# A different form of phi, one load moved behind another, and sums shifted between engines, in a fused linear-attention and SwiGLU kernel

## The chip, the cores and the metric

The kernel runs on one core of one Trainium2 chip. The metric is the device time of one execution in microseconds (us); smaller is better. A profile's *span* is some 1.8 us shorter than the time of the same execution. All runs quoted here are fast (granted TensorE clock 0.995 to 1.0), and every kernel is compared with runs of the kernel before that were taken in the same rounds on the same chip.

Names of engines: PE is the matrix engine, PEld its weight loads, DVE the vector engine, ACT the scalar engine, POOL the general-purpose engine, SP the engine that issues plain DMAs.

## The reference

```python
def phi(x):                       # elu(x) + 1
    return np.where(x > 0, x, np.exp(x) - 1.0) + 1.0
q_p, k_p = phi(q), phi(k)         # q, k, v: [8, 8, 576, 64]
kv  = einsum('bhsd,bhse->bhde', k_p, v)
z   = sum(k_p, axis=2)
num = einsum('bhsd,bhde->bhse', q_p, kv)
den = einsum('bhsd,bhd->bhs', q_p, z)[..., None] + 1e-06
x   = (num / den) as [4608, 512]
out = (silu(x @ w_gate) * (x @ w_val)) @ w_out     # d_ff = 1536
```

The two forms of phi are equal: relu(x) + min(exp(x), 1), and min(max(x, 0) + 1, exp(x)).

## The kernel before

The 4608 tokens are worked through in nine groups of 512 (`g` = 0 to 8), each with a gate/value product (L1) and an output product (L2). Batch b+1's attention is done in the gaps of group b. PE is the engine to keep busy; the rest must be ready in time. Group 0 is special: its weights are still arriving, so its L2 runs in sixteen blocks `i`, each with a third or a sixth of the contraction (`f0` to `f1`), and batch 1's attention is placed between these blocks.

```python
pV = three PSUM banks; pX = three PSUM banks; pG = two PSUM banks     # 512 fp32 columns each

def relu(src, dst, b, lp):        # ACT, 20 of them in batches 3 to 7
    nc.scalar.activation(out=dst..., in_=src..., func=AF.Relu)
def phi_sum(e, dst, b, lp):       # DVE
    nc.vector.tensor_scalar(out=e, in0=e, scalar1=1.0, op0=ALU.min)
    nc.vector.tensor_tensor(out=d, in0=d, in1=e, op=ALU.add)
# batches 1 and 2: max(x, 0) on DVE instead of relu on ACT, so three DVE operations

# the end of the load queue of the first part
    ld_w2(0, 2); ld_w2(2, 4)      # wo, twelve blocks of 128 rows
    ld_v(1)                       # v of batch 1
    ld_w2(4, 8)                   # the third wo load
    ld_w2(8, 12)                  # the fourth

# group 0's L2: block number i, what is done after it
(7, t1(0)), (7, mm1(1, 0)), (7, mm1(1, 1)), (7, num8), (7, r1_copies), (7, x8),
(8, t1(1)), (8, den1(0)), (9, num1(0)), (9, den1(1)), (9, x1(0)), ...
```

Here `t1` transposes batch 1's q, `mm1` is k.v of batch 1, `den1` and `num1` are its denominators and numerators (denominators then go through log and exp on ACT), `num8` and `x8` are the query product and scaling of batch 0's ninth block, and `w_sum` makes sums of wo's quarters (buffer `ws`) for a saving scheme used from group 2 on. `t2` transposes the last two blocks of batch 1's q, `den2` makes their denominators, `r1_copies` copies batch 1's k.v out of PSUM, `x1` scales their outputs, and `joint(2)` is batch 2's k.v with the diagonal for its z product; the *z product* spreads batch 2's sum of phi(k) over the partitions. `den1` writes columns 0 to 447 of banks pX[0] and pX[1]; `num8` writes the last columns of pX[1] and pV[2].

## Time and profile before

| | before, the profiled execution |
|---|---|
| time of that execution | 307.99 us |
| median of the other runs known then | 306.96 us (306.41 to 307.02) |
| PE, DVE, ACT busy | 296.7, 250.5, 213.9 us |
| holes of PE after 16 us | 0.20 us at 40.7, 1.38 us ending at 43.27, 1.08 us ending at 83.68 |

A *hole* is counted in this document as follows: the start of a matmul, less the start of the one before it in order of start, less the streaming time of that one (matmuls of 512 columns that follow each other without a wait start 0.216 us apart). About 0.1 us is normal where the matmul shape changes. Landing times of DMAs are read from the same records.

The page's first part, of the kernel before (busy us, share of the span, instructions):

```profile
PE 296.7 (97%) x2596; PEld 182.0 (59%) x2596; DVE 250.5 (82%) x536; ACT 213.9 (70%) x333; POOL 49.0 (16%) x63
```

The view of PE's waits, of the kernel before (engine, what waited, for what: us in total, times, longest):

```profile
PE pX L596 <- DVE sil L587: 1.3, 1, 1.3
PE pV L450 <- DMA wo<-in_moe_w_out_dram: 1.2, 1, 1.2
PE pX L264 <- DMA qT<-qp: 0.9, 1, 0.9
```

PE has almost no waits. The first is the warm-up at the start. The second is a block of group 0's L2 waiting for the third wo load. The third is group 2's query product waiting for a DMA transpose. The timeline of PE around the second, of the kernel before (start us, us, engine, line, operation):

```profile
41.85 0.19 PE L264 MATMUL pX<-qT,R 64*64 64x64 f16 x1
41.86 0.19 PE L264 MATMUL pV<-qT,R 64*64 64x64 f16 x1
43.27 1.02 PE L450 MATMUL pV<-wo,hT 128*128 128x512 f16 x4 [1.21 <-DMA wo<-in_moe_w_out_dram]
```

Its chain of work that ended last names the two DMAs (start us, us, what):

```profile
26.88 16.34 DMA wo<-in_moe_w_out_dram
...
78.03 5.61 DMA qT<-qp
```

The load was issued at 26.88 and landed at 43.22; the transpose was issued at 78.03 and landed at 83.64.

### The profile page before, as it was taken

Reading aid. Unit: us, or ns where it says so; the run is one execution under the profiler, and the core shown is the slowest. Engines: PE = TensorE matmul, PEld = TensorE weight load, DVE = VectorE, ACT = ScalarE, POOL = GpSimd, SP = SyncE. Lnnn points to the kernel's source line nnn. Section 1 sums busy time; section 2 is a strip of 40 time slices with the busy share of each in tenths; the row PEclk is TensorE's granted clock in tenths of the full one; section 3 lists DMA queues with packets and bytes.
Section 4 is the critical chain, followed back from the end, with each engine's and each line's share of the span. In section 5 each row is a group of like instructions: output and inputs, shape, how many; then the busy total and the mean of one; then the engine's idle time right before and its main releaser. Section 6 shows DMA issues by size and latency. Waiting matters only on the chain.

```text
span 306.2 us, 6694 instructions
## 1 busy us (share of the span) xinstructions
PE 296.7 (97%) x2596; PEld 182.0 (59%) x2596; DVE 250.5 (82%) x536; ACT 213.9 (70%) x333; POOL 49.0 (16%) x63
## 2 busy tenths in 40 slices
PE   8899989999899999999999999999999999999993
PEld 5644444444344486447744774468446878778883
DVE  4754856979967988998899889997999968968891
ACT  4864959869657878696869686968633478547931
POOL 8554259110200002000200000000000003001300
PEclk9999999999999999999999999999999999999998
DMA  7999999999794219921792133132312050023014
GB/s 208 195 196 201 207 207 201 227 217 167 84 241 101 49 30 153 217 53 29 130 234 48 37 70 71 28 54 51 89 26 54 8 132 0 2 66 74 0 37 103
DMA packets 41472, 32.88 MB, mean 107 GB/s; under 512 B 16400, under 2 KB 36816, under 8 KB 41440
## 3 DMA queue, kind: packets, MB, share of 16 engines
q0 software_dynamic: 20176, 18.35, 38.4%
q1 hardware_dynamic: 21104, 13.97, 19.2%
q8 instruction: 20, 0.33, 0.4%
q10 hardware_dynamic: 160, 0.13, 0.2%
q14 instruction: 12, 0.10, 0.1%
HBM read 37.75 MB, written 9.44 MB: 154 GB/s over the span
## 4 chain that ended last, share of the span: by engine, by line
PE 69%; DMA 14%; issue 7%; ACT 4%; DVE 3%; POOL 2%; POOLq 0%; ACTq 0%; DVEq 0%
PE pV L291 17%; PE pG L291 17%; PE pX L506 14%; DMA wo<-in_moe_w_out_dram 5%; PE pV L506 4%; PE pV L343 4%; PE pG L343 4%; DMA wv<-in_moe_w_val_dram 3%; DMA wg<-in_moe_w_gate_dram 3%; PE pG L450 2%; DMA qT<-qp 2%; ACT sil L296 1%; PE pV L450 1%; PE pX L343 1%; PE pV L264 1%
## 5 line engine op out<-in xcount | busy, mean ns | idle before, releaser
L291 PE MATMUL pV<-xT,wv 128*128 128x512 f16 x324 | 83.5, 379 | 0.0
L291 PE MATMUL pG<-xT,wg 128*128 128x512 f16 x296 | 76.3, 379 | 0.0
L297 DVE SCALAR_TENSOR_TENSOR hT<-pV,sil 128x512 f16<-128x512 f32 x81 | 55.1, 686 | 14.3 <-PE pV L291 7.1
L296 ACT ACTIVATE sil<-pG 128x512 f16<-128x512 f32 x74 | 43.5, 596 | 29.7 <-PE pG L291 20.6
L291 PEld LDWEIGHTS <-wv 128*128 128x128 f16 x336 | 32.9, 98 | 39.6
L291 PEld LDWEIGHTS <-wg 128*128 128x128 f16 x336 | 32.5, 98 | 38.4
L506 PEld LDWEIGHTS <-hs 128*128 128x128 f16 x336 | 32.5, 98 | 4.7 <-DVE hs L480 0.4
L383 POOL TENSOR_TENSOR hT<-prod,vm 128x512 f16<-128x512 f16 x6 | 6.9, 1154 | 132.0 <-ACT vm L370 132.0
L506 PEld LDWEIGHTS <-hT 128*128 128x128 f16 x252 | 24.3, 98 | 4.1
L506 PE MATMUL pX<-ws,hs 128*128 128x256 f16 x210 | 25.7, 273 | 0.0
L511 ACT ACTIVATE part<-pX 128x256 f32<-128x256 f32 x35 | 12.8, 381 | 13.2 <-PE pX L506 13.1
L95 POOL DMA_DIRECT2D k<-in_k_dram x7 | 5.4, 772 | 77.0 <-ACT part L511 58.4
L480 DVE TENSOR_TENSOR hs<-hT 128x512 f16<-128x512 f16 (+2 forms) x42 | 17.4, 417 | 0.2
L245 DVE TENSOR_TENSOR qp<-qp,rden 128x768 f16<-128x768 f16 x18 | 17.1, 948 | 0.0
L232 DVE TENSOR_REDUCE den<-prod 128x12 f32<-128x768 f16 x18 | 16.9, 942 | 0.0
L120 ACT ACTIVATE ek<-k 128x1152 f16<-128x1152 f16 x14 | 16.0, 1158 | 0.1
L450 PEld LDWEIGHTS <-hT 128*128 128x128 f16 x96 | 8.7, 98 | 11.6 <-issue 1.8
L506 PE MATMUL pX<-wo,hT 128*128 128x256 f16 x126 | 15.2, 273 | 0.0
L155 ACT ACTIVATE vm<-v 128x1152 f16<-128x1152 f16 x12 | 14.1, 1178 | 0.0
L120 ACT ACTIVATE eq<-q 128x1152 f16<-128x1152 f16 x12 | 13.3, 1169 | 0.0
L450 PE MATMUL pV<-wo,hT 128*128 128x512 f16 x48 | 12.0, 380 | 1.2 <-DMA wo<-in_moe_w_out_dram 1.2
L516 DVE SCALAR_TENSOR_TENSOR osb<-pX,part 128x256 f32<-128x256 f32 x28 | 10.7, 417 | 2.1 <-PE pX L506 1.9
(192 smaller groups left out, 541.4 us busy)
## 6 DMA issues: line engine op xcount, KB each, us to landing
out_dram<-osb SPq DMA_DIRECT2D x64, 128.0 KB, 4.1
k<-in_k_dram POOLq DMA_DIRECT2D x7, 576.0 KB, 8.5
q<-in_q_dram POOLq DMA_DIRECT2D x7, 576.0 KB, 10.5
v<-in_v_dram POOLq DMA_DIRECT2D x7, 576.0 KB, 13.6
wg<-in_moe_w_gate_dram POOLq DMA_DIRECT2D x5, 256.0 KB, 9.1
wv<-in_moe_w_val_dram POOLq DMA_DIRECT2D x5, 256.0 KB, 9.7
wo<-in_moe_w_out_dram POOLq DMA_DIRECT2D x2, 512.0 KB, 16.0
out_dram<-osb SPq DMA_DIRECT2D x13, 64.0 KB, 2.0
```

Source lines behind the costliest of these rows:

```text
L120: nc.scalar.activation(out=e[:, s, :], in_=src[b % 2][:, s, :], func=AF.Exp, bias=0.0, scale=1.0)
L155: nc.scalar.activation(out=vm[b % 2][:, :, s, 0:D].rearrange("p j l d -> p l j d"), in_=v16[b % 2][:, s, :].rearrange("p l (j d) -> p l j ...
L232: nc.vector.tensor_reduce(out=den[:, HL * j0:HL * j1], in_=prod[:, 0:j1 - j0, :].rearrange("p j (l d) -> p (j l) d", d=D), axis=AX.X, op=A ...
L245: nc.vector.tensor_tensor(out=qv, in0=qv, in1=rden[:, HL * j0:HL * j1].unsqueeze(2).to_broadcast([P, HL * (j1 - j0), D]), op=ALU.mult)
L291: nc.tensor.matmul(out=ps[:, :], lhsT=src[:, i, P * fb:P * fb + P], rhs=xT[i][g % 2][:, :], start=(i == 0), stop=(i == 3))
L296: nc.scalar.activation(out=s[:, :], in_=pg[:, :], func=AF.Silu, bias=0.0, scale=1.0)
L297: nc.vector.scalar_tensor_tensor(out=hT[g % 2][:, fb, :], in0=pv[:, :], scalar=SC, in1=s[:, :], op0=ALU.mult, op1=ALU.mult)
L343: nc.tensor.matmul(out=dst[:, HN * e:HN * e + HN], lhsT=lhs, rhs=rhs, start=(n in (1, 2, 5) and e == 0 and c == 0), stop=(c == 1), skip_gr ...
L450: nc.tensor.matmul(out=pso[(g, t)][:, :], lhsT=hT[g % 2][:, fb, P * t:P * t + P], rhs=wo[:, fb, :], start=(fb == 0), stop=(fb == FB - 1))
L480: (eng or nc.vector).tensor_tensor(out=o, in0=a, in1=b, op=op)
L506: nc.tensor.matmul(out=(z if n in (2, 3, 5) else x)[:, 0:HD], lhsT=left(f), rhs=right(f), start=(f == 0 and n in (1, 2, 5)), stop=(f == HF ...
L511: nc.scalar.activation(out=part[:, 2 * i + tt, :], in_=(x if from_x else z)[:, 0:HD], func=AF.Copy, bias=0.0, scale=1.0 / SC)
```

## The change

Its intent: take relu off ACT and one operation off DVE in batches 1 and 2; let the third wo load land before PE wants it, by moving batch 1's v behind it, which means that k.v of batch 1 has to come two blocks later; and take the wo sums out of group 1, where DVE and ACT are full. The diff, cut to its core (its last lines, on the wo sums and on relu, are in words):

```diff
-    def relu(src, dst, b, lp): ...                     # ACT
-    def phi_sum(e, dst, b, lp): ...                    # DVE: min, then add
+    def plus_1(src, dst, b, lp):                       # DVE
+        nc.vector.tensor_scalar(out=dst[...], in0=src[...], scalar1=0.0, scalar2=1.0,
+                                op0=ALU.max, op1=ALU.add)
+    def least(e, dst, b, lp):                          # DVE
+        nc.vector.tensor_tensor(out=d, in0=d, in1=e, op=ALU.min)
...
-            kvb[b] = (..., (pX[1], pV[2]), ...         # banks of batch 1's k.v
+            kvb[b] = (..., (pX[2], pV[2]), ...
...
+    ld_w2(4, 8)
     ld_v(1)
-    ld_w2(4, 8); ld_w2(8, 12)
+    ld_w2(8, 12)
...
-    num8_out = [(pX[1], pV[2])[m % 2][:, 3 * P:4 * P][:, part8[m]] for m in range(4)]
+    num8_out = [pV[2][:, 0:C], pX[1][:, W7:W7 + C], pV[2][:, C:2 * C], pX[0][:, W7:W7 + C]]
...
-  (7, t1(0)), (7, mm1(1, 0)), (7, mm1(1, 1)), (7, num8), (7, r1_copies), (7, x8),
-  (8, t1(1)), (8, den1(0)), (9, num1(0)), (9, den1(1)), (9, x1(0)), (11, t2), ...
+  (7, t1(0)), (8, t1(1)), (8, den1(0)), (8, num8), (8, x8), (9, mm1(1, 0)), (9, mm1(1, 1)),
+  (9, den1(1)), (9, r1_copies), (10, num1(0)), (10, x1(0)), (10, w_rest), (12, t2), ...
...
-  wo sums: POOL at block 4 (0:2) and 8 (2:4), all four; DVE in group 1 (4:6)
+  wo sums: POOL at block 4 (0:2), all four; DVE at block 10 (2:6), m = 2, 0 (w_rest);
+           POOL at block 12 (2:6), m = 1, 3
-  group 1 on: relu_k, relu_q on ACT in slots 4 to 7
```

Constants: P = 128, C = 64, W7 = 448.

More of the change, by code (lines that the diff above doesn't have):

```diff
@@ L120, in exp_, with phi @@
         nc.scalar.activation(out=e[:, s, :], in_=src[b % 2][:, s, :], func=AF.Exp, bias=0.0, scale=1.0)
-    def relu(src, dst, b, lp):
-        s = slice(2 * lp, 2 * lp + 2)
-        nc.scalar.activation(out=dst[b % 2][:, :, P * lp:P * lp + P].rearrange("p j (s d) -> p s j d", d=D),
-                             in_=src[b % 2][:, s, :].rearrange("p s (j d) -> p s j d", d=D),
-                             func=AF.Relu, bias=0.0, scale=1.0)
-    def relu_k(b, lp):
-        relu(k16, kp, b, lp)
-    def relu_q(b, lp):
-        relu(q16, qp, b, lp)
-    def phi_sum(e, dst, b, lp):
-        s = slice(2 * lp, 2 * lp + 2)
-        nc.vector.tensor_scalar(out=e[:, s, :], in0=e[:, s, :], scalar1=1.0, scalar2=None, op0=ALU.min)
+    def plus_1(src, dst, b, lp):
+        nc.vector.tensor_scalar(
+            out=dst[b % 2][:, :, P * lp:P * lp + P].rearrange("p j (s d) -> p s j d", d=D),
+            in0=src[b % 2][:, 2 * lp:2 * lp + 2, :].rearrange("p s (j d) -> p s j d", d=D), scalar1=0.0, scalar2=1.0,
+            op0=ALU.max, op1=ALU.add)
+    def least(e, dst, b, lp):
         d = dst[b % 2][:, :, P * lp:P * lp + P].rearrange("p j (s d) -> p s j d", d=D)
-        nc.vector.tensor_tensor(out=d, in0=d, in1=e[:, s, :].rearrange("p s (j d) -> p s j d", d=D), op=ALU.add)
+        nc.vector.tensor_tensor(out=d, in0=d, in1=e.rearrange("p s (j d) -> p s j d", d=D), op=ALU.min)
+    def phi(src, e, dst, b, lp):
+        plus_1(src, dst, b, lp)
+        least(e[:, 2 * lp:2 * lp + 2, :], dst, b, lp)
     def exp_k(b, lp):
@@ L146, in phi_k @@
     def phi_k(b, lp):
-        phi_sum(ek, kp, b, lp)
+        phi(k16, ek, kp, b, lp)
     def phi_q(b, lp):
-        phi_sum(eq, qp, b, lp)
+        phi(q16, eq, qp, b, lp)
     def vcast(b, lp):
@@ L167, in mm1 @@
         if lp == 0:
-            kvb[b] = ((pV[2], pX[0]), (pX[1], pV[2]), (pX[0], pX[1]), (pV[0], pG[0]), (pX[2], pV[2]))[min(b, 4)]
+            kvb[b] = ((pV[2], pX[0]), (pX[2], pV[2]), (pX[0], pX[1]), (pV[0], pG[0]), (pX[2], pV[2]))[min(b, 4)]
         for j in range(J):
@@ L731 @@
         ld_w2(2 * i, 2 * i + 2)
+    ld_w2(4, 8)
     ld_v(1)
-    for i in range(1, 3):
-        ld_w2(4 * i, 4 * i + 4)
+    ld_w2(8, 12)
     ld_k(2)
@@ L742, in at @@
         return sl
-    def phi_1(e, dst, lp):
-        nc.vector.tensor_scalar(out=e, in0=e, scalar1=1.0, scalar2=None, op0=ALU.min)
-        d = dst[1][:, :, P * lp:P * lp + P].rearrange("p j (s d) -> p s j d", d=D)
-        nc.vector.tensor_tensor(out=d, in0=d, in1=e.rearrange("p s (j d) -> p s j d", d=D), op=ALU.add)
     def t1(lp):
@@ L815, in k_block @@
             exp_(k16, ek, 1, lp)
-            term(k16[1], kp[1], lp, 0.0, ALU.max)
+            plus_1(k16, kp, 1, lp)
         for lp in range(2):
-            phi_1(ek[:, 2 * lp:2 * lp + 2, :], kp, lp)
+            least(ek[:, 2 * lp:2 * lp + 2, :], kp, 1, lp)
     def q_block():
@@ L824, in q_block @@
             nc.scalar.activation(out=es[lp], in_=q16[1][:, 2 * lp:2 * lp + 2, :], func=AF.Exp, bias=0.0, scale=1.0)
-            term(q16[1], qp[1], lp, 0.0, ALU.max)
+            plus_1(q16, qp, 1, lp)
         z0_copy(1, 0)
@@ L828, in q_block, with w_rest @@
         for lp in range(2):
-            phi_1(es[lp], qp, lp)
-    def max_2(src, dst, lp):
-        term(src[0], dst[0], lp, 0.0, ALU.max)
+            least(es[lp], qp, 1, lp)
+    def w_rest():
+        for m in (2, 0):
+            w_sum(nc.vector, m, 2, 6)
     def first():
@@ L836, in first @@
         w = at(17, [
-            (3, lambda: z0(1, 0)), (3, lambda: z0(1, 1)), (3, q_block), (7, lambda: t1(0)), (7, lambda: mm1(1, 0)),
-            (7, lambda: mm1(1, 1)), (7, lambda: num8()), (7, lambda: r1_copies()), (7, lambda: x8()), (8, lambda: t1(1)),
-            (8, lambda: den1(0)), (9, lambda: num1(0)), (9, lambda: den1(1)), (9, lambda: x1(0)), (11, lambda: t2()),
-            (11, lambda: num1(1)), (11, lambda: x1(1)), (12, lambda: exp_k(2, 0)), (12, lambda: den2()),
-            (15, lambda: max_2(k16, kp, 0)), (15, lambda: max_2(k16, kp, 1)), (14, lambda: num2()),
-            (14, lambda: exp_k(2, 1)), (14, lambda: exp_q(2, 0)), (15, lambda: exp_q(2, 1)), (16, lambda: x2()),
-            (16, lambda: phi_k(2, 0)), (16, lambda: phi_k(2, 1))])
+            (3, lambda: z0(1, 0)), (3, lambda: z0(1, 1)), (3, q_block), (7, lambda: t1(0)), (8, lambda: t1(1)),
+            (8, lambda: den1(0)), (8, lambda: num8()), (8, lambda: x8()), (9, lambda: mm1(1, 0)), (9, lambda: mm1(1, 1)),
+            (9, lambda: den1(1)), (9, lambda: r1_copies()), (10, lambda: num1(0)), (10, lambda: x1(0)), (10, w_rest),
+            (12, lambda: t2()), (12, lambda: num1(1)), (12, lambda: x1(1)), (13, lambda: exp_k(2, 0)), (13, lambda: den2()),
+            (14, lambda: num2()), (14, lambda: exp_k(2, 1)), (14, lambda: exp_q(2, 0)), (15, lambda: exp_q(2, 1)),
+            (16, lambda: x2()), (16, lambda: phi_k(2, 0)), (16, lambda: phi_k(2, 1))])
         return sl, w
@@ L863, in steady @@
         if b == 2:
-            items = [(0, lambda: vcast(2, 0)), (1, lambda: vcast(2, 1)), (1, lambda: max_2(q16, qp, 0)), (1, lambda: phi_q(2, 0)),
-                     (2, lambda: max_2(q16, qp, 1)), (2, lambda: phi_q(2, 1)), (3, lambda: joint(2))] + items
+            items = [(0, lambda: vcast(2, 0)), (1, lambda: vcast(2, 1)), (1, lambda: phi_q(2, 0)),
+                     (2, lambda: phi_q(2, 1)), (3, lambda: joint(2))] + items
         elif b == 3:
@@ L907 @@
     for (i, (t, f0, f1)) in enumerate([(t, f0, f1) for (f0, f1) in ((0, 2), (2, 4), (4, 8), (8, 12)) for t in range(4)]):
-        if i in (4, 8):
+        if i == 4:
             for m in range(4):
-                w_sum(nc.gpsimd, m, i // 2 - 2, i // 2)
+                w_sum(nc.gpsimd, m, 0, 2)
+        if i == 12:
+            for m in (1, 3):
+                w_sum(nc.gpsimd, m, 2, 6)
         l2(0, t, f0, f1)
@@ L929 @@
             for lp in range(2):
-                sl[4 + lp].append(lambda lp=lp: relu_k(b2, lp))
-                sl[6 + lp].append(lambda lp=lp: relu_q(b2, lp))
                 sl[8 + lp].append(lambda lp=lp: vcast(b2, lp))
@@ L935 @@
         for m in range(4):
-            if g == 1:
-                sl[3 + m].append(lambda m=m: w_sum(nc.vector, m, 4, 6))
-            else:
+            if g > 1:
                 sl[3 + m].append(lambda m=m: h_sum(g, m, 0, 2))
```

## The prediction

> **What bounds it.** The page shows PE busy 97% of 306.2 us at a granted clock of 0.996. Comparing matmul starts in the trace, PE is packed from 16 to 295 us, apart from pauses of 0.1 us where the shape changes. Three real holes are left: 0.20 us at 40.7 (first transpose of batch 1's q, waiting for its phi), 1.38 us ending at 43.27 (the wait view: PE pV L450 for DMA wo; the third wo load lands at 43.22 because batch 1's v, issued ahead of it, took the queue until 40.36), and 1.08 us ending at 83.68 (query product of group 2, waiting for a DMA transpose issued at 78.03, landed at 83.64). So about 2.66 us is all there is to gain; from group 2 on there is nothing.
>
> **Costs.** Relu on ACT: 20 x 1.155 us = 23 us removed. On DVE, min (0.45) plus add (0.76) becomes max-and-add plus min. The Trainium skill ("VectorE: DVE Perf Modes", perf-mode tier table) puts fp16 tensor_scalar in the 4x tier and tensor_tensor in the 2x tier; this trace agrees (1152 elements: 0.45 and 0.76 us, strided max included). I expect 0.45 and 0.76 again, so steady DVE time is unchanged. In batches 1 and 2 three DVE ops become two: eight times 0.45 us saved. wo sums: eight POOL ops of 1.15 us and four DVE ops of 0.42 us (group 1) become four short and two double POOL ops (2.3 us each, estimate) and two double DVE ops (0.7 us each, estimate), now inside group 0's output product.
>
> **Critical path.**
> 1. The third wo load should land near 40.4, v near 43.2, the fourth wo unchanged near 45.5. PE reaches the third block at about 41.0, k.v at about 43.6, the fourth block at about 46.8: none waits. Gain 1.4, plus 0.2 for the earlier phi.
> 2. Given back: the DVE sums sit ahead of the copy of the last two transposed blocks (den2 may wait 0.3 us), and group 1's k.v may wait 0.2 us for the cast of v on ACT.
> 3. The hole at 83.68: without relu and sums in group 1, DVE and ACT keep up; the second transpose is issued near 76.4. The load of batch 5's k, which collided with it (issued 79.33, freed by the exp), now also waits for max-and-add, issued near 81-82. The transpose should take about 2.9 us like the first, landing near 79.5, before PE needs it (about 81.4). Gain 1.08.
>
> Net: 1.6 + 1.1 - 0.5 = 2.2 us.
>
> **Prediction:** 304.8 us, range 303.8 to 306.2. Faster by over 2%: 0.01; within 2%: 0.98; slower: 0.01.
>
> **What would show it.** Right: no PE wait on wo; third wo landing before 41; group 1's first gate matmul near 51.8 instead of 53.08; query product of group 2 without a hole; groups 2 to 7 unchanged at 31.5 us each; ACT busy down by about 23 us to 191; DVE busy down by about 4 us. Wrong: new PE waits around 43 (v), 46-50 (den2, x), 58-59 (k.v of batch 2), or the transposes still 5 us long.
>
> **What would make it wrong.** Two-op tensor_scalar leaving the fast tier (over 0.8 us each), which would crowd DVE (18 of 20 us busy in the steady groups) and stall PE everywhere; POOL sums running longer and delaying batch 3's loads; the hole at 83.68 moving rather than closing, which leaves a gain of 1.1 us.

## The result, and the profile after

The changed kernel took 307.28 us (median of 4 runs, 307.11 to 307.38) against 306.99 us (4 runs). Ratios here are the mean time of one kernel's fast runs over that of the other's of the same rounds, so not quite the ratio of the medians: 1.0012, interval 0.9994 to 1.0029. Two later sessions gave 1.0019 (1.0005 to 1.0033) and 1.0006 (0.9987 to 1.0024). The change is worth nothing, or costs a tenth of a per cent. The predicted 2.2 us are absent.

The page's first part, of the changed kernel:

```profile
PE 296.4 (97%) x2596; PEld 181.5 (59%) x2596; DVE 247.5 (81%) x526; ACT 193.4 (63%) x313; POOL 49.2 (16%) x61
```

ACT lost 20.5 us and DVE 3.0 us, about as foreseen, and PE is as busy as ever. (The twenty relus lasted 23.1 us in sum, as predicted; busy time counts only once where two records of an engine overlap.) The views by line that show the cost of phi (line, engine, operation, shapes, times | busy us, mean ns | idle before), of the kernel before and then of the changed one:

```profile
L136 DVE TENSOR_SCALAR ek<-ek 128x1152 f16<-128x1152 f16 x12 | 5.5, 457 | 5.1 <-ACT ek L120 5.1
L138 DVE TENSOR_TENSOR kp<-kp,ek 128x1152 f16<-128x1152 f16 x12 | 9.1, 759 | 0.4
L603 DVE TENSOR_SCALAR qp<-q 128x1152 f16<-128x1152 f16 x5 | 2.2, 453 | 0.0
L124 ACT ACTIVATE kp<-k 128x1152 f16<-128x1152 f16 x10 | 11.6, 1157 | 0.0
```

```profile
L123 DVE TENSOR_SCALAR qp<-q 128x1152 f16<-128x1152 f16 x14 | 6.2, 452 | 0.0
L130 DVE TENSOR_TENSOR kp<-kp,ek 128x1152 f16<-128x1152 f16 x14 | 10.6, 758 | 5.4 <-ACT ek L120 5.0
```

L603 is max alone, L123 max-and-add. The view of PE's waits, of the changed kernel:

```profile
PE pX L592 <- DVE sil L583: 1.3, 1, 1.3
PE pX L260 <- ACT rr L655: 1.2, 1, 1.2
```

Both waits for DMAs are gone. In their place stands a wait of 1.2 us for ACT. The timeline of PE there, of the changed kernel:

```profile
42.50 0.38 PE L260 MATMUL pX<-qT,zz 64*64 64x448 f16 x4
42.72 0.19 PE L260 MATMUL pV<-qT,R 64*64 64x64 f16 x1
44.14 0.19 PE L260 MATMUL pX<-qT,R 64*64 64x64 f16 x1 [1.24 <-ACT rr L655]
```

and of ACT:

```profile
42.93 1.16 ACT L655 ACTIVATE rr<-pX,epst 128x448 f32<-128x448 f32 x2 [0.66 <-PE pX L260]
```

At 42.50 the denominators (`den1(0)`) are written to columns 0 to 447 of pX[0] and pX[1]. At 42.72 the first matmul of `num8` goes to pV[2]. The second goes to column 448 and up of pX[1], and it starts only at 44.14, just after ACT's two logs have read pX[0] and pX[1] (42.93 to 44.09). No byte is shared. The hole is 1.40 us, against the 1.38 us that the load order removed.

Two smaller holes came with it: 0.28 us at 51.0 (`den2` behind the copy that DVE makes after `w_rest`, as predicted) and 0.28 us at 64.8 (batch 2's z product). The hole ahead of group 2's query product is gone, as predicted. And yet the trace is only 0.7 us shorter than the first trace of before, and the times are not shorter at all. So two questions are open: is the new wait the bank, and what is the hole at 83.68 worth?

The load of batch 5's k was later, as predicted. POOL's timelines, of the kernel before and then of the changed one:

```profile
79.33 0.74 POOL L95 DMA_DIRECT2D k<-in_k_dram  x1 [15.75 <-ACT ek L120]
```

```profile
82.25 0.74 POOL L95 DMA_DIRECT2D k<-in_k_dram  x1 [17.93 <-DVE kp L123]
```

In the changed kernel the second transpose was issued at 77.26 and landed at 80.15, before that load started. Not foreseen: the first of these transposes now took 5.3 us (72.08 to 77.40) instead of 2.9, in all three traces of the changed kernel 5.3 to 5.6 us, and the third 2.7 us instead of 6.7. Slow transposes were among the prediction's signs of being wrong; this one held PE up in none of these traces.

### The profile page after: what moved, and what is told of

The parts are those of the page before. It is cut to its first block, busy times and chain, and to the rows that moved or that the text cites. A ratio compares the mean times of both kernels' runs of the same rounds, so it can differ in the third digit from the quotient of the medians.

```text
span 305.5 us, 6677 instructions
## 1 busy us (share of the span) xinstructions
PE 296.4 (97%) x2596; PEld 181.5 (59%) x2596; DVE 247.5 (81%) x526; ACT 193.4 (63%) x313; POOL 49.2 (16%) x61
## 4 chain that ended last, share of the span: by engine, by line
PE 89%; issue 5%; DMA 2%; ACT 1%; DVE 1%; POOL 0%; POOLq 0%; DVEq 0%; ACTq 0%
PE pV L287 23%; PE pG L287 21%; PE pX L502 14%; PE pV L502 4%; PE pV L339 4%; PE pG L339 4%; PE pV L446 3%; PE pX L287 3%; PE pG L446 3%; DMA q<-in_q_dram 2%; PE pV L260 1%; PE pX L260 1%; PE pX L339 1%; PE pX L177 1%; PE pV L407 1%
## 5 line engine op out<-in xcount | busy, mean ns | idle before, releaser
L130 DVE TENSOR_TENSOR kp<-kp,ek 128x1152 f16<-128x1152 f16 x14 | 10.6, 758 | 5.4 <-ACT ek L120 5.0
```

## The experiments

Theory A: the first gain was swallowed by `num8`'s wait for the bank; the second hole was for the most part peculiar to the execution that was profiled, whose time (307.99 us) was 1.0 us over the others. Rivals: the second hole is in every execution and its closing was given back elsewhere (B); PE would have waited near 43 us anyway, for v or for the transposed q (C).

### The kernel before, a second trace (e0_before)

No edit.

> The kernel before, unchanged: a second trace of it. Its first trace came from an execution of 307.99 us, 1.0 us over the median of its other runs. Theory A (the hole of 1.08 us before the query product of group 2 was mostly an accident of that execution): the time is near 307.0 and that hole is below 0.3 us in the new trace; the hole of 1.4 us at the third wo load is there again. Rival B (the hole belongs to every execution, and the change gave its closing back somewhere else): the hole is again about 1.1 us, at a time near 307.0.

It took 306.62 us (5 runs), ratio 0.9994 to the kernel before in the same rounds, which it is. The view of PE's waits:

```profile
PE pV L450 <- DMA wo<-in_moe_w_out_dram: 1.1, 1, 1.1
```

The wait for qT is not in the list: the second transpose, issued at 77.49, landed at 80.57, although the load of k was issued 1.3 us after it, as before. The hole for wo is 1.26 us. Theory A's half on the second hole holds for this trace.

### num8 back ahead of the denominators (e1_num8)

```diff
-    num8_out = [pV[2][:, 0:C], pX[1][:, W7:W7 + C], pV[2][:, C:2 * C], pX[0][:, W7:W7 + C]]
+    num8_out = [(pX[1], pV[2])[m % 2][:, 3 * P:4 * P][:, part8[m]] for m in range(4)]
-  (7, t1(0)), (8, t1(1)), (8, den1(0)), (8, num8), (8, x8), ...
+  (7, t1(0)), (7, num8), (7, x8), (8, t1(1)), (8, den1(0)), ...
```

> The changed kernel with the query product of batch 0's last block (and its scaling) put back to where it was, ahead of the denominators of batch 1, in its old banks. Theory A (the change lost its first gain to this product's wait of 1.4 us for the log on ACT that reads the same bank): no PE hole over 0.3 us between 38 and 46 us, first gate matmul of group 1 near 52.0 instead of 53.34, time 1.2 to 1.4 us under the changed kernel, about 306.0. Rival C (PE would have waited there anyway, for v or for the transposed q): the hole moves to the k.v or the denominators of batch 1 and the time stays near 307.2.

306.22 us, ratio 0.9981 (0.9969 to 0.9994). The hole is gone and nothing took its place before 50 us. The timeline of PE, of this kernel:

```profile
41.69 0.19 PE L260 MATMUL pX<-qT,R 64*64 64x64 f16 x1
41.70 0.19 PE L260 MATMUL pV<-qT,R 64*64 64x64 f16 x1
41.82 1.04 PE L446 MATMUL pV<-wo,hT 128*128 128x512 f16 x4
42.69 0.55 PE L743 MATMUL pX<-id,qp 128*128 128x128 f16 x7
43.18 0.38 PE L260 MATMUL pX<-qT,zz 64*64 64x448 f16 x4
43.49 1.04 PE L446 MATMUL pG<-wo,hT 128*128 128x512 f16 x4
```

Rival C falls. Group 1's first gate matmul came at 52.51 (near 52.0 was expected). About 1 us came off the changed kernel (307.28, and 307.10 in the next session), a little under what was expected.

### The new phi alone (e2_phi) and the new load order alone (e3_load)

```diff
 # e2_phi, on the kernel before: relu, phi_sum and the batch 1 and 2 forms replaced by plus_1 and least
 # e3_load, on the kernel before: the load order, banks and places of mm1, den1, num1, t2 of the change;
 #   num8 and x8 left at block 7; relu, min and the wo sums left as they were
```

> The kernel before with the new phi alone (loads, order and wo sums as before). If relu on ACT and the early release of k cost PE time (rival B), the hole before group 2's query product closes and the time falls by about 1.1 us to 305.9. If that hole is an accident (theory A), the time is within 0.3 us of the kernel before; the hole of 1.4 us at the third wo load stays either way.

306.32 us, ratio 0.9986 (0.9973 to 1.0). The second hole is absent, which says little, since it was absent from e0_before as well. More telling is the first: the hole for wo was only 0.54 us, because PE came to it later (1.4 us was expected). The third wo load landed at 42.82, about as in e0_before (42.69), but the first wo matmul of this trace started at 36.97 instead of 35.91. A hole that ends at a DMA's landing shrinks by about as much as PE is late: of the 1.06 us, 0.20 us was made up where the wait for batch 1's phi(q) is gone, and the load landed 0.13 us later; the hole shrank by the other 0.72 us.

> The kernel before with the load order and the later k.v alone, but with batch 0's last query product left ahead of the denominators; relu and the wo sums as before. Theory A: the hole of 1.4 us at the third wo load is gone and nothing takes its place before 46 us. If the gain survives to the end, the time is about 1.2 us under the kernel before (305.8); if the later part of group 1, which needs ACT with relu in it, gives it back, a hole opens before group 2's query product and the time stays near 307.0.

306.42 us, ratio 0.999 (0.9978 to 1.0003). The hole at the third wo load is gone; group 1 started at 51.49 us, 1.06 us before that of e0_before, of which 0.33 us was an earlier start of group 0 (14.25 against 14.58). It was given back. The timeline of PE, of this kernel:

```profile
63.51 0.38 PE L212 MATMUL pX<-zd,ones 128*128 128x512 f16 x1 [0.68 <-ACT R L196]
```

This is batch 2's z product, a hole of 0.84 us; a further 0.38 us went at group 2's query product, whose transpose took 4.9 us. Group 2 then began at 85.92, against 85.87 in e0_before. With three DVE operations per phi and relu on ACT, the other engines set the pace of group 1. So each half alone is worth about a tenth of a per cent, at the edge of what five rounds resolve.

### The changed kernel again (e7_after), and num8 in another bank (e6_px2)

```diff
 # e7_after: no edit.  e6_px2, on the changed kernel:
-    num8_out = [pV[2][:, 0:C], pX[1][:, W7:W7 + C], pV[2][:, C:2 * C], pX[0][:, W7:W7 + C]]
+    num8_out = [pV[2][:, 0:C], pX[2][:, W7:W7 + C], pV[2][:, C:2 * C], pX[2][:, 0:C]]
```

> The changed kernel, unchanged: a second trace and five more times. In the three traces with the new phi (changed kernel, num8 moved back, phi alone) the load of the second half of batch 0's q landed at 8.3 to 8.5 us, in the three with the old phi at 7.3 to 7.9 us, with the same issue time, and the first gate matmul came 0.1 to 1.1 us later. If that belongs to the kernel, the new trace has it near 8.4 again and the time is near 307.2; if it is chance between executions, it may land anywhere from 7.3 to 8.5. The hole of 1.4 us at batch 0's last query product is there in either case.

307.10 us, ratio 1.0019 (1.0005 to 1.0033); the hole is 1.40 us again. The q load landed at 8.03.

> The changed kernel with the two parts of batch 0's last query product that go to the banks of batch 1's denominators sent to the third bank (the one of the transposed q) instead, in the same place of the program. Theory A (the wait is for whoever still reads the bank that it writes): it waits for the copy of the transposed q on DVE, which ends about 0.5 us after the denominators begin, instead of both logs on ACT; the hole shrinks from 1.4 to about 0.4 to 0.6 us and the time falls by about 0.9 us. Rival (it waits for its operands): the hole stays 1.4 us.

306.26 us, ratio 0.9986 (0.9973 to 1.0). The timeline of PE, of this kernel:

```profile
42.62 0.19 PE L260 MATMUL pV<-qT,R 64*64 64x64 f16 x1
43.20 0.19 PE L260 MATMUL pX<-qT,R 64*64 64x64 f16 x1 [0.38 <-DVE qT L748]
```

The hole fell from 1.40 to 0.54 us, by 0.85 us, and the time in the same session from 307.10 to 306.26 us, by 0.84 us. The operands and the place in the program are the same; only the bank differs, and with it the engine waited for: DVE, which copies columns 0 to 447 of pX[2]. The first matmul that waited writes columns 448 and up, which DVE does not read. This settles it: the wait is for the reader of the bank. It is a semaphore wait in the program, on that matmul, for ACT in the changed kernel.

The Trainium skill ("PSUM — Partial Sum Buffer", section "PSUM bank collisions raise a hardware error") says why a program has such waits: two engines may not touch the same bank and quadrant of partitions at once, disjoint columns included, so it gives the rule to guard PSUM by bank and not by address. This agrees as far as a run without a race can: both placements waited for the whole bank.

### Later wo sums and a later phi(q) (e4_wlate, e9_phiq, e10_best, e11_pad)

```diff
 # e4_wlate, on e1_num8
-  (10, x1(0)), (10, w_rest), ... (13, den2), ...
+  (10, x1(0)), ... (13, den2), (13, w_rest), ...
 # e9_phiq, on e4_wlate: batch 2 in group 1
-  (1, phi_q(2, 0)), (2, phi_q(2, 1)), (3, joint(2))
+  (1, phi_q(2, 0)), (3, joint(2)), (4, phi_q(2, 1))
 # e10_best, on e9_phiq: POOL's sums behind the sum they read
-        if i == 12: POOL w_sum, m = 1, 3
+        if i == 14: POOL w_sum, m = 1, 3
 # e11_pad, on e10_best: twenty relus of one column on ACT in the slots of the old relus
```

> The changed kernel with the query product put back (as in the run before that did so) and the wo sums on DVE moved behind the copy of the last two transposed blocks. The hole of 0.28 us ahead of the last denominators of batch 1 closes; the time falls by 0.2 to 0.3 us against the run with the query product alone, if PE's lead is not given back at batch 2's z product (hole of 0.28 us at 64 us, which then grows to about 0.5).

> As the one with later wo sums, and the second half of batch 2's phi(q) also moved behind the k.v of batch 2 and its diagonal. If the hole at batch 2's z product comes from DVE doing phi(q) ahead of the diagonal, it closes (below 0.15 us), and no PE hole over 0.2 us is left between 17 and 295 us. The time is then 0.5 us under the run with the query product alone, about 305.7.

Both gave a wrong result (relative error 17.9), by my mistake: POOL's sums read one that DVE makes, and I had moved DVE's behind them in the program. Their times (306.37 and 305.79 us) belong to no usable kernel. Their traces still show two things about PE: with the sums out of the way the hole at `den2` closed, and in e9_phiq the hole at the z product closed too.

> The last kernel made right: the two runs with later wo sums gave a wrong result because the sums on POOL, which read a sum made on DVE, stayed ahead of it in the program; here they come behind it. Expected: correct, no PE hole over 0.2 us between 17 and 285 us, 305.8 us, 0.7 us (0.2%) under the kernel before and 1.3 us under the changed kernel.

Correct, but 306.46 us, ratio 0.9987 (0.9972 to 1.0002): a miss. A new hole of 1.10 us opened at 58.96 us. The timeline of DVE and then of POOL, of this kernel:

```profile
54.51 2.56 DVE L130 TENSOR_TENSOR kp<-kp,ek 128x1152 f16<-128x1152 f16 x1
57.00 0.45 DVE L123 TENSOR_SCALAR kp<-k 128x1152 f16<-128x1152 f16 x1
57.55 0.76 DVE L130 TENSOR_TENSOR kp<-kp,ek 128x1152 f16<-128x1152 f16 x1
```

```profile
52.03 4.43 POOL L482 TENSOR_TENSOR ws<-wo,ws 128x1024 f16<-128x1024 f16 x2 [6.09 <-DVE ws L482]
```

The same DVE operation took 2.56 us while POOL's two sums ran (to 56.46) and 0.76 us right after; e11_pad shows the same again (2.56 us, with a hole of 1.10 us). DVE was 1.8 us late and PE waited for it. The Trainium skill ("GPSIMD Engine Reference", section "Specifications") states that POOL shares its SBUF interfaces with DVE and contends with DVE instructions that have two SBUF inputs; this trace agrees, and adds the size. In the changed kernel POOL's double sums ran from 50.09 to 54.43, while DVE read PSUM for the most part, in its usual times (0.61 us for a scaling of 448 columns, 0.68 us for a copy of 512). The first such DVE operation came at 55.44: it was clear of this by a microsecond. The timelines of POOL and DVE, of the changed kernel:

```profile
50.09 4.34 POOL L482 TENSOR_TENSOR ws<-wo,ws 128x1024 f16<-128x1024 f16 x2 [4.02 <-DVE ws L482]
55.44 0.76 DVE L130 TENSOR_TENSOR kp<-kp,ek 128x1152 f16<-128x1152 f16 x1
```

> The same with twenty one-column relus on ACT where the old phi had its relus, so that ACT has as many instructions as before and none of its work. If the late landing of the first q load in kernels with the new phi (seven traces: 8.0 to 8.6 us; three with the old: 7.3 to 7.9) comes from the shorter ACT program, it lands at 7.3 to 7.9 here and the first wo matmul comes near 36.0; the time falls by 0.5 us. If it does not depend on the program, the landing is as likely anywhere in 7.3 to 8.6.

306.57 us, ratio 0.999 (0.9975 to 1.0006); q landed at 8.44. The number of ACT instructions does not bring an early landing.

### The changed kernel without its wo sums (e5_phi_load), and the kernel before again (e12_before)

```diff
 # e5_phi_load: e2_phi and e3_load together, i.e. the change with num8 at block 7 and the old wo sums
 # e12_before: no edit
```

> The kernel before with the new phi and the new load order, the query product of batch 0 in its old place and the wo sums as before: the change without its third part and without its misplaced product. If the wo sums on DVE in group 0 cost the 0.28 us ahead of the last denominators, that hole is absent here. The hole at batch 2's z product (0.28 us) stays. Expected time 0.2 to 0.3 us under the run with the product alone put back.

305.85 us, ratio 0.9965 (0.9948 to 0.9983): with e13_best below, the fastest. The hole at `den2` is absent, as expected, so the redistributed sums were what cost 0.28 us there. PE has one hole over 0.13 us between 17 and 290 us, 0.28 us at the z product.

> The kernel before once more, for a third trace. The first load of q lands below 8.0 us if that goes with the kernel. The hole at the third wo load is 1.2 to 1.4 us; the hole ahead of group 2's query product is anything from 0 to 1.1 us (first trace 1.08, second below 0.13), depending on whether the load of batch 5's k, issued 1.3 us after the second transpose, catches it.

The profiled execution took 308.51 us, and its view of PE's waits is:

```profile
PE pX L264 <- DMA qT<-qp: 1.4, 1, 1.4
PE pV L450 <- DMA wo<-in_moe_w_out_dram: 1.3, 1, 1.3
```

with this piece of the chain that ended last:

```profile
78.06 6.11 DMA qT<-qp
```

So the second hole is real, but it comes and goes: here 1.57 us, with the transpose at 6.1 us. The other five times of this kernel in the session were 306.46, 306.60, 306.77, 306.96 and 307.89 us.

### Last runs (e13_best, e14_after, e15_before)

```diff
 # e13_best, on e5_phi_load: phi_q(2, 1) behind joint(2), as in e9_phiq.  e14_after, e15_before: no edit
```

> The fastest version so far (new phi, new load order, query product of batch 0 in its old place, wo sums as before) with the second half of batch 2's phi(q) behind the k.v of batch 2. The hole of 0.28 us at batch 2's z product closes and no PE hole over 0.2 us is left; the time falls by 0.2 to 0.3 us, to about 0.4 per cent under the kernel before. If another wait takes its place, the time stays at 0.35 per cent under.

305.85 us, ratio 0.9962 (0.9946 to 0.9978). The hole at the z product is closed; the trace has one of 0.21 us left at 35.78 (PE waits for the first wo load) and none over 0.2 us after it. The time did not fall visibly against e5_phi_load, which ran in another session with the same median; 0.28 us is below what this comparison resolves.

> The changed kernel for the third time: hole of 1.40 us at batch 0's last query product again, none ahead of group 2's query product, times within 0.6 us of each other, about 307.2. The q load lands between 8.0 and 8.6 us if lateness goes with the kernel, and anywhere above 7.3 if not.

306.93 us, ratio 1.0006 (0.9987 to 1.0024); hole of 1.40 us at `num8`, 0.28 us at `den2`, 0.28 us at z, none at group 2's query product. Five of six times lie between 306.59 and 306.95 us, one at 307.90 us, so the spread was wider than expected. q landed at 8.14.

> The kernel before for the fourth time: hole of 1.2 to 1.5 us at the third wo load; the hole ahead of group 2's query product between 0 and 1.6 us; times with a wider spread (0.7 to 2 us) than the changed kernel's, median 306.8. The q load lands between 7.3 and 8.1 us.

306.87 us. Hole for wo 1.27 us; no hole at the query product. The times range from 306.43 to 307.69 us. q landed at 8.32, outside what was expected. Over all traces it landed between 7.43 and 8.57 us with the new phi (12 traces) and between 7.34 and 8.32 us with the old (5 traces). The suspicion that the changed kernel loads later did not hold: the ranges overlap almost wholly, and the landing varies between executions by about a microsecond with the issue time unchanged at 1.37 us. Why it varies is open.

### The ledger

Start of the first gate matmul of groups 0 to 3, and the span, in us:

| trace | group 0 | group 1 | group 2 | group 3 | span |
|---|---|---|---|---|---|
| before, first | 15.07 | 53.08 | 87.50 | 119.05 | 306.22 |
| before, e15_before | 15.20 | 53.10 | 86.41 | 117.95 | 305.09 |
| changed, first | 15.31 | 53.34 | 86.93 | 118.39 | 305.47 |
| changed, e14_after | 15.01 | 53.04 | 86.61 | 118.08 | 305.17 |
| e5_phi_load | 14.73 | 51.37 | 84.95 | 116.41 | 303.53 |
| e13_best | 14.31 | 51.16 | 84.47 | 115.93 | 303.38 |

From group 0 to group 1 the kernel before needs 37.90 us (e15_before) and the changed one 38.03 us (e14_after): 1.27 and 0.20 us of holes went, 1.40 and 0.28 us came. From group 1 to group 2 it is 33.31 and 33.57 us: the hole at the z product came, and in this execution of before there was no hole at the query product to close. The first trace of before, in which there was one, needs 34.42 us. From the start of group 3 to the end all six need 187.1 to 187.5 us. With `num8` where it was and the old wo sums, the first stretch is 36.64 us (e5_phi_load).

## Why the prediction was right or wrong, point by point

- *What bounds the kernel, and that nothing is to be gained from group 2 on:* right. From the start of group 2's gate product to that of group 3 it is 31.5 us before and after, and the same for groups 3 to 5. The prediction's "31.5 us each" was wrong for groups 6 and 7: they take 30.8 and 28.6 us, also before and after.
- *Costs:* right. max-and-add took 0.45 us on average for q and 0.48 us for k (0.45 us in the median; one of fourteen took 0.79 us), min 0.76 us; before, min took 0.45 and add 0.76 us, and max alone 0.45 us. So the second ALU operation was nearly free; this agrees with the tier that the prediction took from the Trainium skill ("VectorE: DVE Perf Modes", perf-mode tier table; the table's column is bf16, and the page's conditions for these modes name any 16-bit type). ACT fell to 193.4 us (191 predicted), DVE busy time by 3.0 us (4 predicted). POOL's double sums took 2.13 us each (2.3 estimated), DVE's 0.68 us (0.7).
- *Third wo load near 40.4, v near 43.2, fourth near 45.5:* right: 40.09, 43.49, 45.54.
- *"PE reaches the third block at about 41.0, k.v at about 43.6, the fourth block at about 46.8: none waits. Gain 1.4":* **this is the step that failed.** None of those three waited, but the product between them did. I had checked that each matmul's operands and columns were free. The diff moved `num8` behind `den1(0)` and into the same banks; e1_num8 and e6_px2 show that the 1.40 us is the wait for the bank's reader. The Trainium skill states the rule, in the section on PSUM bank collisions named above, and I had not applied it.
- *Given back, 0.3 us at `den2`:* right, 0.28 us; e5_phi_load shows that it comes with the redistributed sums.
- *Given back, 0.2 us at k.v of batch 2 for the cast of v:* about the right size and slightly wrong in place: 0.28 us at the z product after it, behind phi(q) on DVE (it closes in e13_best, where only that order was changed).
- *"Gain 1.08" at 83.68:* **the second step that failed, in its size.** The mechanism holds as far as it was seen: in every trace with the new phi the k load was issued later, and none has this hole. That the k load is what slows the transpose is not shown: with the same issue times (78.03 and 79.3) the transpose took 5.61 us in the first trace of before and 2.88 us in e15_before. But the hole is not a property of the kernel. It was 1.08, under 0.13, 1.57 and under 0.13 us in four traces of before; the two with it came from executions of 307.99 and 308.51 us, the two without from 306.35 and 306.86 us. What a median over runs had to give here was probably little; how many of the executions without a trace had the hole is not known. The warning was on the first page: the profiled execution was 1.0 us slower than the median of the others.
- *The sum:* predicted -1.6 - 1.1 + 0.5 = -2.2 us. In e14_after and e15_before it is -1.27 - 0.20 + 1.40 + 0.28 in the first part and +0.28 in group 1, about +0.5 us of holes; the two spans differ by 0.08 us, because the executions also differ in where they start and in pauses too short to be counted.
- *The part of the gain that was there:* with the misplaced product put back and the old wo sums, the change's other two parts together give 0.35% or 1.06 us (e5_phi_load, 0.9965; 0.17 to 0.52%), of the 2.2 us predicted, while each of them alone gives about 0.1%. These figures alone do not exclude a plain sum (0.14 and 0.10%); the traces show why it may be more. The load order alone gives its lead back in group 1 (e3_load), and the new phi alone leaves the hole at the wo load.

What stays open: why the first loads and the transpose vary between executions.

## What to carry to other kernels

When work is moved, ask for each PSUM access who else has that bank open at its new place, not only whether its columns and operands are free; a wait for two ACT operations (1.16 us together) ate what a better load order gave. Before a hole in a trace is counted as a gain, look at whether the profiled execution is a typical one of its kernel, and take a second trace if it is slower than the median by about the size of the hole. A lead won on the critical engine must be carried by the others through the next stage, so a load order and a lighter phi that are each worth a tenth of a per cent may be worth more together than their sum (0.35% here, not resolved from the sum by these runs).

## What the Trainium skill lacked or had wrong

- "GPSIMD Engine Reference" (Specifications) says that POOL and DVE contend where DVE has two SBUF inputs, and gives no size; neither does any other page for this pair of operations: a DVE tensor_tensor of 1152 fp16 elements took 2.56 us instead of 0.76 us while two POOL tensor_tensor operations of 1024 elements ran.
- No page that I read says how much the same DMA varies between executions: over the 17 traces of these kernels the first load of q landed between 7.34 and 8.57 us with the issue at 1.37 us (7.68 to 8.32 us in four traces of the kernel before), and the same transpose took 2.9 to 6.1 us in four traces of one kernel.
